# A new order for the steps behind the first 300, and a new deal of the PSUM banks, in linear attention with an MLP behind it

## Chip, cores, metric

The kernel runs on one core of one Trainium2 chip. The metric is the device time of one execution in microseconds, as a median of runs.

## What is computed

Softmax attention in its linear form, `q` over its feature axis and `k` over the sequence, for 8 batches of 8 heads, 576 positions of 64 features. Its output, as 4608 tokens of 512 features, goes through an MLP of width 2048 whose activation is `h * tanh(softplus(h))` (Mish). All in fp32.

```python
q_s = exp(q - max(q, -1)); q_s = q_s / (sum(q_s, -1) + 1e-09)
k_s = exp(k - max(k, 2));  k_s = k_s / (sum(k_s, 2) + 1e-09)
kv = einsum('bhsd,bhse->bhde', k_s, v)
attn = einsum('bhsd,bhde->bhse', q_s, kv)
x = attn.transpose(0, 2, 1, 3).reshape(4608, 512)
h = x @ w_in                                    # 512 x 2048
g = h * tanh(log1p(exp(minimum(h, 20.0))))
out = g @ w_out                                 # 2048 x 512
```

## The kernel before

Two heads make one item of 128 partitions, so there are 32 items, four to a batch. Every operand of the large matmuls is split into a high and a low part of a shorter fp32 form, and a product is three matmuls (high x high, high x low, low x high). All large matmuls have 128 rows, 128 columns of weights and 512 columns of data.

What is run, and when, stands in one string, `ORDER` (line 23): 2522 steps, each a name with numbers. Line 991 walks over it and calls the function that the table `stages` gives for the name. Scheduling is by hand, so each engine runs its instructions in the order of the steps, and waits by semaphores for what its next instruction reads, or for a buffer's last reader. `BANKS` (line 156) holds one letter for each PSUM tile in the order in which the steps allocate them; the letter names one of eight banks.

The steps that matter here, by engine:

- TensorE. `H n` (`h_part`, line 623): three matmuls of the first MLP product for one batch; `HM n`: four of these. `O`, `OP n.t` (`out_part`, line 667): three matmuls of the second MLP product into `po`. `A k.n.p` (`first_product`, line 815) and `BB k.f.p` (`second_product`, line 827): six matmuls each of the first and second MLP product for pairs of batches, in a form with seven products in place of eight (p = 1 to 7), into tiles `px`, `py`, `pz` and `qx`, `qy`, `qz`. `PX`, `PK`, `KP`, `XP`, `XT`, `T0` to `T7`: the small matmuls of the attention.
- VectorE. `RB`, `RC`: bit operations that decode the weights. `RD j`: the low part of a weight (`wi`, `wo`), a 128x512 subtract with both inputs in SBUF; `GL`: the same for `g`, with an input in PSUM. `WW`, `WL` (`w_whole`, line 720, `w_mix_lo`, line 745): adds and subtracts in SBUF that make mixed weights. `MK`, `MQ`, `Q`: maxima and sums of k and q; `KS`: the subtract of k's maximum; `U`, `T8` and up: transposes; `MT`, `KM`, `QV`: short steps in SBUF between them, `S`: the scaled `kv`. `GX`, `GK` (lines 872, 891), `XA`, `XL` (line 793): 128x1024 subtracts in SBUF that mix the data of the second form and make its low parts; a `BB` needs its `GK`, an `A` its `XL`. `J`, `DJ`: 128x512 adds out of PSUM.
- ScalarE. Exponentials, Mish, copies out of PSUM and all high parts (`RH`, `WH`, `GH`, `XH`, `C`, `N`, `Y`, `GM`, `EQ` and others).
- GpSimd. `SQ i`, `QM i` (lines 395, 494): q less its maximum, q times the inverse of its sum. `RO j`: low parts of weights, the rest that `RD` leaves. `RL`: a scaling; `WM` (line 728): mixed weights. `F e` (`w_fetch`, line 801): the DMA that fetches one tile of mixed weights for two products `A` or `BB`, 200 in all.
- SyncE issues all other DMAs: loads (`L`, `LK`, `LQ`, `V`, `R`), mixed weights to DRAM (`WK`, `WP`), and stores (`ST`, `ES`, `DS`, `DT`).

A fetch goes into one of six buffers in turn:

```python
RING = ["w0", "w1", "xa0", "xa1", "xa2", "xa3"]
tag = {2: "w14", 3: "w15"}.get(e, RING[(e - LEAD) % 6])
```

so `F e` waits, on GpSimd's queue, until the products of fetch e - 6 have been done, and all that stands behind it on that queue waits with it.

Of the kernel before, what the change touches and what calls it, by code (L numbers as in the profile page):

```python
# [47 lines left out]
GM20 WH13.1 MS10 T9 WL13.0 WL13.1 WW14v MT10 LK12 WP13.0 WP13.1 SQ10 WM14.0p WM14.1p PX8 PK8 Z9 Z8 EQ10 EV0.1s ZL9 S10
EV0.2v ZL8 Q10 MK12 QW10 WH14.0 ZT9 EV0.3s WH14.1 KB12 WK4 LQ11 QV10 WL14.0 WL14.1 KM12 MQ11 V12 WK12 WP14.1 WP14.0
WK13 WK14 HM30 HM26 HM31 HM16 HM18 HM17 HM22 MS11 UE12.0 QM10 T10 MT11 U12.0 WW15v SQ11 WM15.0p WM15.1p UE12.1 EQ11  # L50
Q11 QW11 GM30 GM26 WH15.0 WH15.1 ZT8 GM18 GM22 QV11 U12.1 WL15.0 WL15.1 LQ12 LK14 WP15.0 WP15.1 QM11 T11 WW0v WM0.0p
PX10 PK10 HM19 Z10 Z11 GM31 WM0.1p ZL11 ZL10 S12 MQ12 GM16 GM17 WH0.1 MS12 WH0.0 WL0.1 WL0.0 MK14 WW1v MT12 V14 ES0.2
# [1007 lines left out]
```

## Time and profile before

| | us |
|---|---|
| median of 3 runs (lowest, highest) | 795.55 (794.21, 798.1) |
| profiled execution | 794.31 |
| its span, first to last instruction | 792.5 |
| TensorE busy in it | 775.1 |
| VectorE, ScalarE, GpSimd busy | 565.6, 511.0, 295.1 |

TensorE ran at its full granted clock throughout. The profile is read from the waits of TensorE back: which wait ended last, which engine or DMA released it, and what stood in that engine's queue before. Busy shares are averages over stages with different limits. A large matmul is listed with some 0.39 us, but one follows the other every 0.23.

### The profile page before, as it was taken

What the parts mean: (1) busy time and instruction counts of PE and PEld (TensorE: products, weight loads), DVE (VectorE), ACT (ScalarE), POOL (GpSimd) and SP (SyncE); (2) the same over time, 40 slices, a digit from 0 to 9 for tenths busy, and PEclk for the clock granted to TensorE, in tenths of its full rate; (3) what the DMA queues carried; (4) which work ended last, traced back from release to release, by engine and by line L of the source; (5) the groups of instructions that cost most, each with busy time, mean ns of one, the idle gap of its engine ahead of it and who ended that gap; (6) DMA issues with size and microseconds to landing.
All of it is one profiled execution on the core that took longest, in us unless ns stands there. A gap on an engine that the chain in (4) does not pass through costs nothing.

```text
span 792.5 us, 12626 instructions
## 1 busy us (share of the span) xinstructions
PE 775.1 (98%) x4592; PEld 624.0 (79%) x4592; DVE 565.6 (71%) x877; ACT 511.0 (64%) x952; POOL 295.1 (37%) x378
## 2 busy tenths in 40 slices
...
GB/s 342 396 350 224 192 244 205 325 341 247 204 165 233 300 371 229 334 246 258 187 265 230 241 279 196 273 167 225 166 251 212 207 244 159 213 176 199 236 190 208
DMA packets 80717, 192.75 MB, mean 243 GB/s; under 512 B 16016, under 2 KB 28560, under 8 KB 80656
## 3 DMA queue, kind: packets, MB, share of 16 engines
...
q10 hardware_dynamic: 144, 0.13, 0.0%
...
## 4 chain that ended last, share of the span: by engine, by line
PE 68%; DVE 7%; DMA 7%; issue 2%; ACT 2%; POOL 1%; SPq 0%; POOLq 0%; ACTq 0%; DVEq 0%
PE px L823 14%; PE qx L839 13%; PE ph L629 11%; PE qz L839 9%; PE qy L839 8%; PE py L823 7%; PE pz L823 3%; DMA ws<-ws 3%; DVE gs L224 2%; DMA q<-in_qs_dram 2%; PE pt L573 1%; DVE g L224 1%; PE px L538 1%; PE po L670 1%; DMA xt_dram<-xt 1%
## 5 line engine op out<-in xcount | busy, mean ns | idle before, releaser
L807 POOL DMA_DIRECT2D ws<-ws x200 | 108.0, 542 | 350.1 <-PE qx L839 92.4
L224 DVE TENSOR_TENSOR gs<-g,gs 128x1024 fp32r<-128x1024 f32 x112 | 137.7, 1243 | 37.6 <-ACT gs L889 33.7
L889 ACT CAST gs<-g 128x1024 fp32r<-128x1024 f32 x112 | 116.7, 1051 | 62.8 <-PE qx L839 24.4
L839 PE MATMUL qx<-gs,ws 128*128 128x512 f32 x576 | 135.6, 391 | 0.4 <-DMA ws<-ws 0.4
L823 PE MATMUL px<-xh,ws 128*128 128x512 f32 x384 | 128.9, 393 | 2.6 <-DMA ws<-ws 2.4
L839 PEld LDWEIGHTS qx<-gs,ws 128*128 128x128 f32 x576 | 107.7, 188 | 24.8 <-DMA ws<-ws 0.8
L839 PE MATMUL qz<-gs,ws 128*128 128x512 f32 x384 | 92.0, 391 | 1.8 <-DVE gs L224 1.8
L629 PE MATMUL ph<-xs,wi 128*128 128x512 f32 x384 | 91.0, 393 | 1.3 <-DVE gl L224 1.0
L839 PE MATMUL qy<-gs,ws 128*128 128x512 f32 x384 | 90.8, 390 | 0.0
L859 ACT COPY g<-px 128x512 f32<-128x512 f32 x72 | 41.3, 586 | 76.0 <-PE px L823 68.2
L823 PEld LDWEIGHTS px<-xh,ws 128*128 128x128 f32 x384 | 72.1, 188 | 22.0 <-ACT g L859 2.3
L839 PEld LDWEIGHTS qz<-gs,ws 128*128 128x128 f32 x384 | 71.7, 188 | 18.8 <-DVE gs L224 2.2
L629 PEld LDWEIGHTS ph<-xs,wi 128*128 128x128 f32 x384 | 71.3, 188 | 19.0 <-DVE gl L224 1.4
L224 DVE TENSOR_TENSOR g<-g,g 128x1024 f32<-128x1024 f32 x64 | 78.6, 1241 | 9.1 <-ACT g L867 4.9
L839 PEld LDWEIGHTS qy<-gs,ws 128*128 128x128 f32 x384 | 72.0, 188 | 15.0
L823 PE MATMUL px<-xl,ws 128*128 128x512 f32 x192 | 74.9, 390 | 0.7 <-DVE xl L224 0.7
L863 DVE TENSOR_TENSOR g<-py,g 128x512 f32<-128x512 f32 x48 | 32.0, 681 | 56.3 <-ACT g L859 35.0
L823 PE MATMUL py<-xh,ws 128*128 128x512 f32 x192 | 65.9, 391 | 0.0
L224 POOL TENSOR_TENSOR q<-q,qm 128x576 f32<-128x576 f32 (+1 forms) x31 | 40.5, 1305 | 42.6 <-issue 18.4
L867 ACT ACTIVATE g<-g 128x512 f32<-128x512 f32 x72 | 43.1, 630 | 14.8 <-DVE g L863 14.6
L496 POOL TENSOR_TENSOR qe<-qe,qs 128x576 f32<-128x576 f32 x24 | 30.7, 1281 | 38.6 <-DVE qs L492 32.0
L629 PE MATMUL ph<-xs_odd,wi 128*128 128x512 f32 x192 | 44.9, 391 | 0.0
...
## 6 DMA issues: line engine op xcount, KB each, us to landing
ws<-ws POOLq DMA_DIRECT2D x197, 512.0 KB, 4.7
...
raw_out<-in_w_dram SPq DMA_DIRECT2D x14, 512.0 KB, 7.3
...
```

The costliest lines, as they stand in the source:

```text
L224: eng.tensor_tensor(out, a, b, ALU.subtract)
L496: eng.tensor_tensor(q2, q2, z.unsqueeze(2).to_broadcast(list(q2.shape)), ALU.mult)
L538: nc.tensor.matmul((px, pt)[x][h][o], kvt[a, j], at[e + j]["qT"][x][a], start=True, stop=True)
L573: nc.tensor.matmul(pkv[i][j * D:(j + 1) * D], k, v_two[a, j, c], start=c == 0, stop=c == NR - 1)
L629: nc.tensor.matmul(gs[n], wi[f][:, a, t], x[:, z], start=t == 0 and i == 0, stop=t == HP - 1 and i == 2)
L807: nc.gpsimd.dma_start(dst, src)
L823: nc.tensor.matmul(dst, w[:, a, j], xc[k, p][z][:, j].rearrange("p b s -> p (b s)"), start=p in (1, 2, 7) and j == 0 and i == 0, stop=j == ...
L839: nc.tensor.matmul(psb[key, k][m], w[:, a, m], g[z][:, f % 2], start=first and i == 0, stop=f == NH - 1 and i == 2, skip_group_check=p in ...
L859: nc.scalar.copy(g_quad(k, n)[q], psb[1, k, n])
L863: nc.vector.tensor_tensor(g, psb[2 if q == 0 else 7, k, n], g, ALU.add)
L867: nc.scalar.activation(g, psb[1, k, n] if q == 1 else g, AF.Mish)
L889: nc.scalar.copy(t[0], gq[k, h][G_PART[p]])
```

## The change

The first 300 steps of `ORDER` stay. The 2222 steps behind them, which begin at 57 us of the profiled execution, are the same steps in a new order, on every engine. The letters of `BANKS` are dealt anew from the 75th on, to go with that order. Nothing else differs: no step is added, removed or put on another engine. The order comes from a planner outside the kernel; here it was made anew with other assumptions: when VectorE and GpSimd want the port that they share, it goes to who asks first, and fetches are taken to land later.

The lines of the diff that hold the steps spoken of below:

```diff
--- before.py
+++ after.py
@@ -31,132 +31,132 @@
...
 RO13 RA17 RA14 RS17 RO12 QZ4 O3 RB14 RB17 Y5 RL23 GA5 RC17 Y6 RC14 RL19 GA6 H28 GL5 R25 O4 RS18 RA16 GL6 RA15 RH14
-RB16 RA18 RO14 R31 H29 H30 H31 RM21 QZ5 RC16 RB15 RC15 RH16 RA19 RA21 RH15 RH17 R26 RB19 RB21 RC19 QM4 RO16 RO17 QM5
...
-ZT5 RA27 RM27 Y9 GA9 RO25 WM8.0p RL28 WM8.1p GL10 RB27 GL9 RC27 MQ6 MK7 MK6 H44 H45 H46 H48 H47 H49 O7 B6 H50 H51 O8
-WH8.0 RH22 RH27 RA28 WH8.1 Y11 GA11 WL8.0 WL8.1 RD22 RB28 RC28 GL11 KS6 MQ7 WW9v WK6 WP8.0 LK8 WP8.1 RO26 RO27 SQ6 SQ7
...
-WK11 WP9.0 WP9.1 WK10 RO28 QM6 QM7 WM10.0p WM10.1p H52 H53 O9 H54 H55 H56 H57 H58 H59 O10 RW30 RH29 Y14 Y13 GA13 KB8
...
-WH11.1 Z6 Z7 U8.1 MT8 WL11.0 ZL7 WL11.1 ZL6 SQ8 RH30 EQ8 ST6 LK10 WP11.0 LQ9 WP11.1 ST5 ST7 RD30 Q8 WW12v MQ9 MK10
...
-KM10 MT9 WL12.0 QM8 SQ9 RO31 T8 UE10.1 UE10.0 EQ9 V10 WP12.0 WP12.1 LQ10 U10.0 Q9 WW13v QW9 OP14.0 HM28 HM20 HM23
...
-QV15 MT16 MK18 BB0.4.7 BB0.5.7 BB0.6.7 BB0.7.7 F14 F16 QM15 SQ16 F17 F15 T15 GK0.6.0 WL3.1 GX0.2.2v GX0.3.2v EQ16
-GH0.6.1 KB18 GH0.6.3 GH0.6.2 LQ17 WP3.0 V16 WP3.1 ST12 GK0.6.1 KM18 GX0.2.3v GK0.6.2 GK0.6.3 MQ17 Q16 DJ0.0.0 PX14
-BB0.0.6 BB0.1.6 BB0.2.6 BB0.3.6 BB0.4.6 GH0.3.0 XR14 GH0.5.0 XR15 UE18.1 QW16 MS17 UE18.0 BB0.5.6 BB0.6.6 PK14 BB0.7.6
-QV16 MT17 GK0.5.0 GK0.3.0 U18.0 F20 F19 F18 WM4.0p WM4.1p F22 F21 QM16 SQ17 GH0.5.1 DP0.2.0 DP0.2.1 ZT14 WH4.0 U18.1
...
-XL1.7 S20 XL1.2 XA1.3v XL1.6 A1.0.7 A1.1.7 A1.0.2 A1.0.6 F35 F37 F34 F36 DJ0.2.0 MQ20 WL5.1 XL1.5 WL5.0 DJ0.2.1 WP5.0
-WP5.1 DS0.2.1 DS0.1.0 DS0.3.1 DS0.0.1 DS0.2.0 PS C1.1.0 ZT19 XH1.4 MS20 C1.0.2 A1.1.2 A1.1.6 A1.2.1 A1.0.5 A1.2.2
-J1.1.0 MK22 J1.0.0 XL1.4 MT20 SQ20 F39 F38 C1.1.2 N1.1.0 KB22 C1.0.3 C1.2.0 EQ20 J1.2.0 J1.0.3 KM22 LQ21 A1.0.3 A1.1.5
...
-J2.0.0 QV28 XL2.6 MK30 XA2.3v XL2.5 BB1.5.4 A2.0.7 A2.1.1 BB1.6.4 BB1.7.4 A2.0.6 F90 QM28 F91 MS29 C2.1.0 XH2.4 KB30
-C2.0.2 A2.1.6 A2.1.2 A2.0.5 A2.1.7 DJ1.2.0 MT29 DJ1.2.1 T28 XL2.4 KM30 J2.1.0 SQ29 F92 F95 F94 F93 UE30.1 C2.1.2
...
-C3.0.2 F146 F144 F143 A3.1.2 BB2.6.4 A3.1.1 BB2.7.4 A3.0.5 F147 F145 F148 F150 F149 DJ2.2.1 DJ2.2.0 DJ2.1.1 DS2.2.0
-DS2.2.1 DS2.1.1 DS2.3.1 DS2.3.0 DS2.1.0 C3.1.0 C3.0.3 A3.2.1 A3.1.7 A3.1.6 A3.0.3 C3.2.0 C3.1.2 A3.1.5 A3.2.6 A3.2.2
...
-DS3.1.0 DS3.1.1 DS3.3.0 DS3.2.0 DT3.2.1.0
+RB16 RA18 RO14 RC16 RB15 RC15 H29 RH17 RA19 RM21 RH16 RH15 RA21 H30 H31 O5 RO17 RO16 RB19 RB18 RC19 RB21 RC18 RC21
...
+Y10 RM27 ZT5 ZT4 RA27 G10 GL10 RB27 MQ7 RC27 SQ6 WM8.0p WM8.1p SQ7 WH8.0 RH26 Y9 GA9 WH8.1 RH27 RH25 H44 H45 H46 B6
+H47 H48 WL8.1 WL8.0 KS6 GL9 RD22 WW9v R29 R28 LK8 ST5 WK1 WK10 WP8.0 WP8.1 WK3 WK9 RO25 RL28 RO26 WM9.0p WM9.1p RO27
+Y11 GA11 RA28 EQ6 EK6 EQ7 RA29 RM29 MK8 GL11 RB28 RC28 RB29 Q6 QZ6 Q7 O8 H49 O9 H50 H51 H52 H56 H57 H53 H54 H55 H58
+H59 O10 RH28 WH9.0 Y12 WH9.1 QZ7 WL9.0 RC29 WL9.1 WK11 WP9.0 WP9.1 RW30 KB8 RH29 GA12 Y13 GA13 Y14 GA14 KM8 WW10v GL12
+GL13 GL14 QM7 RO28 QM6 WM10.0p WM10.1p KP6 XP4 UE8.0 RW31 WH10.0 WH10.1 S6 U8.0 O11 T7 O12 WL10.0 WL10.1 RB30 RC30
+RB31 RC31 V8 WK4 WP10.0 WP10.1 LQ8 TC7 Z5 Z4 RH30 RD29 ZL5 ZL4 WW11v RD30 MQ8 T6 WM11.0p TC6 UE8.1 OP13.3 OP13.0 XP6
...
+Q8 WW12v OP14.3 OP13.2 OP13.1 H60 H61 OP14.2 PK6 OP14.1 HM23 H62 H63 QW8 Y15 GM23 QV8 S8 MK10 MQ9 WM12.0p WM12.1p QM8
...
+Q9 QW9 U10.0 QV9 U10.1 MQ10 WM13.0p QM9 WM13.1p HM19 HM24 OP14.0 HM28 HM20 OP15.2 OP15.3 OP15.0 OP15.1 PA WH13.0 GM28
...
+BB0.4.1 PK12 PX12 BB0.5.1 BB0.6.1 BB0.7.1 BB0.0.2 BB0.1.2 F7 SQ15 QM14 F8 F9 F10 GH0.2.1 GH0.2.2 XR13 XR12 S14 U16.0
...
+ES0.1 MK18 GX0.0.2v GK0.7.2 QV15 MQ16 KB18 ZT12 DP0.0.0 ZT13 WH3.1 DP0.0.1 GH0.7.3 MS16 F14 F13 WM4.0p QM15 DJ0.0.0
+GK0.7.3 GX0.3.2v MT16 WL3.1 T15 GX0.1.2v SQ16 F15 F16 EQ16 GH0.6.0 GH0.6.1 WH4.0 Q16 GK0.6.0 GX0.2.2v ST13 DS0.0.0
+WP3.1 ST12 LQ17 ES0.2 BB0.4.7 BB0.5.7 BB0.6.7 BB0.7.7 PX14 BB0.0.6 BB0.1.6 QW16 GH0.6.3 GH0.6.2 XR15 XR14 GH0.3.0 QV16
+GX0.3.3v GK0.6.1 GK0.6.3 DJ0.0.1 MQ17 GK0.6.2 KM18 PK14 BB0.2.6 BB0.3.6 BB0.4.6 BB0.5.6 UE18.0 UE18.1 GH0.5.0 ZT14
+MS17 GH0.5.1 F17 F19 F18 QM16 GX0.0.3v S16 GX0.2.3v GK0.3.0 MT17 GK0.5.0 T16 U18.0 U18.1 BB0.6.6 BB0.7.6 BB0.0.3 F20
+F21 F22 SQ17 WM4.1p F23 DP0.2.0 EQ17 DP0.2.1 ST14 LQ18 LK20 V18 BB0.1.3 BB0.0.5 BB0.1.5 Q17 GK0.5.1 WW5v BB0.2.5 WH4.1
...
+BB0.6.3 BB0.7.3 BB0.0.4 F26 F29 F28 F27 QM18 ZT17 MS19 XR16 XR17 ZT16 GH0.4.1 BB0.1.4 MT19 U20.0 U20.1 T18 GK0.4.1
+SQ19 BB0.2.4 GH0.4.2 EQ19 XH1.1 BB0.3.4 Q19 GK0.4.2 BB0.4.4 QW19 QV19 F31 QM19 F30 F33 F32 DJ0.1.0 S18 T19 PX18 XR19
...
+A1.0.1 BB0.5.4 BB0.6.4 BB0.7.4 A1.1.1 ZT19 XH1.7 XH1.2 C1.0.0 XH1.3 MK22 S20 XL1.7 XL1.3 XA1.2v XL1.2 KB22 ZT18 C1.1.0
+XH1.5 XH1.6 A1.0.7 A1.1.7 A1.1.2 A1.0.2 WM5.0p F35 F34 F37 WM5.1p XA1.3v XL1.6 KM22 DJ0.2.1 MQ20 XL1.5 A1.1.6 A1.0.6
...
+MS29 QW28 DJ1.2.0 KM30 XL2.4 MT29 DJ1.2.1 QV28 A2.1.6 A2.1.2 A2.1.7 A2.0.5 C2.1.2 UE30.0 C2.0.3 A2.1.5 A2.0.3 A2.2.1
+QM28 F93 SQ29 F94 F95 J2.0.3 T28 DJ1.1.1 J2.1.0 N2.0.1 C2.1.3 EQ29 C2.2.0 DS1.1.1 DS1.1.0 LQ30 ST26 A2.0.4 A2.2.2
...
+C3.0.2 C3.1.0 F144 F147 F145 F149 F146 F148 DJ2.2.1 DJ2.1.1 DJ2.2.0 XL3.5 DS2.1.1 DS2.3.0 DS2.2.0 DS2.1.0 DS2.2.1
...
 
 BANKS = """
-abcdefghadbcefga hebcfbagehdgabcg ehfdabchfbeahcfb hgdeaefcacaeaeae fcefecfaecaeface fefefaceefceafca eaefcaecfeaacefb
-aecbgfhedcbahdgb fcegbfadcfabhebc fegdhabcdfcbahah ahgehegfdaehgfcb fgbadghcafbdedef gcdabchfgaedfhga gaagbcagedbgfhbc
-fadaegacbadgfdcb bebfghcaedhcagfb echdbadeghdgbcfa cghghfdage
+abcdefghadbcefga hebcfbagehdgabcg ehfdabchfbeahcfb hgdeaefcacaeaeae fcefecfaecfcecea fecceacafeafceac fcfaecffcaeacefe
+cfbhgebfdcefbgdh caefdfcebgbhcedb ghfdeacgbhgceaae aedfdfbaehfdabcg aefhfgbcbehdbagh dfcabgecfdhdecaf faafbggbfahbecdh
+gfcagbegdfehcdge fabfgchaedahahbf gdcechfgabdecfhe fbgeadbfhg
```

## Rows read from the trace of the kernel before

**Rows 1.** The page: busy time of each engine, share of the span, instructions.
```profile
PE 775.1 (98%) x4592; PEld 624.0 (79%) x4592; DVE 565.6 (71%) x877; ACT 511.0 (64%) x952; POOL 295.1 (37%) x378
```

**Rows 2.** TensorE's waits: who waited for whom, total us, times, longest us.
```profile
PE px L823 <- DMA ws<-ws: 2.4, 2, 1.5
...
PE ph L629 <- DVE gl L224: 1.0, 1, 1.0
...
PE pq L515 <- DVE gl L224: 0.2, 1, 0.2
```

**Rows 3.** Windows: stretch, its length, busy us of each engine, clock, DMA.
```profile
57.40:121.30 63.90, 60.01 (x416) 45.25 (x415) 58.59 (x96) 49.42 (x95) 42.75 (x39) 1.00 0.67 229
234.70:318.70 84.00, 80.88 (x579) 63.35 (x578) 79.27 (x125) 56.90 (x114) 34.08 (x47) 1.00 0.84 280
```

**Rows 4.** VectorE's timeline, first stretch: start, us, line, operation, tiles, [idle before].
```profile
83.63 3.46 DVE L224 TENSOR_TENSOR m_out<-m_out 128x512 fp32r<-128x512 f32 x2 [0.37 <-POOL m_out L739]
87.01 1.75 DVE L224 TENSOR_TENSOR wo<-wc_out,wo 128x512 fp32r<-128x512 f32 x1
...
90.61 1.34 DVE L224 TENSOR_TENSOR k<-k,pb 128x1152 f32<-128x1152 f32 x1
91.87 0.81 DVE L392 TENSOR_REDUCE qm<-q 128x10 f32<-128x640 f32 x1
...
120.58 0.68 DVE L224 TENSOR_TENSOR wo<-wc_out,wo 128x512 fp32r<-128x512 f32 x1
```

**Rows 5.** GpSimd's timeline, first stretch.
```profile
84.80 1.74 POOL L224 TENSOR_TENSOR wi<-wc_in,wi 128x512 fp32r<-128x512 f32 x1
86.50 1.71 POOL L224 TENSOR_TENSOR q<-q,qm 128x640 f32<-128x640 f32 x1
```

**Rows 6.** VectorE's timeline, second stretch.
```profile
267.24 4.69 DVE L224 TENSOR_TENSOR gs<-g,gs 128x1024 fp32r<-128x1024 f32 x2
...
315.08 1.22 DVE L224 TENSOR_TENSOR xl<-raw,xh 128x1024 fp32r<-128x1024 f32 x1
```

**Rows 7.** GpSimd's timeline, second stretch.
```profile
268.54 1.18 POOL L496 TENSOR_TENSOR qe<-qe,qs 128x576 f32<-128x576 f32 x1
269.66 1.17 POOL L224 TENSOR_TENSOR q<-q,qm 128x576 f32<-128x576 f32 x1
```

**Rows 8.** TensorE's timeline where it had stood.
```profile
261.27 5.74 PE L839 MATMUL qx<-gs,ws 128*128 128x512 f32 x24 [0.40 <-DMA ws<-ws]
...
271.98 2.79 PE L839 MATMUL qz<-gs,ws 128*128 128x512 f32 x11 [1.83 <-DVE gs L224]
...
318.74 0.50 PE L823 MATMUL px<-xl,ws 128*128 128x512 f32 x1 [0.72 <-DVE xl L224]
...
497.56 0.47 PE L823 MATMUL px<-xh,ws 128*128 128x512 f32 x1 [0.92 <-DMA ws<-ws]
...
651.56 0.50 PE L823 MATMUL px<-xh,ws 128*128 128x512 f32 x1 [1.45 <-DMA ws<-ws]
```

**Rows 9.** TensorE's timeline, the first matmuls of `O9` and of `OP14.0`.
```profile
92.24 0.62 PE L670 MATMUL po<-wo,gh 128*128 128x512 f32 x2
...
124.46 0.62 PE L670 MATMUL po<-wo,gh 128*128 128x512 f32 x2
```

**Rows 10.** The chain that ended last: start, us, what; 36 matmuls without a break.
```profile
125.30 8.16 PE ph L629 x36
```

**Rows 11.** Groups by shape, 57 to 322 us: `MK`, xcount, busy us, mean ns, idle before.
```profile
L373 DVE TENSOR_REDUCE km<-kt_two 128x4 f32<-128x1152 f32 x7 | 9.3, 1329 | 0.0
```

**Rows 12.** GpSimd's timeline, the fetches F15, F93 and F149 (each last of its row).
```profile
254.04 1.12 POOL L807 DMA_DIRECT2D ws<-ws  x2
...
490.20 0.53 POOL L807 DMA_DIRECT2D ws<-ws  x1 [0.26 <-issue]
...
643.71 1.06 POOL L807 DMA_DIRECT2D ws<-ws  x2 [3.55 <-PE px L823]
```

**Rows 13.** The page's DMA issues: operation, count, KB each, median us to landing.
```profile
ws<-ws POOLq DMA_DIRECT2D x197, 512.0 KB, 4.7
```

More of the change, by code (lines that the diff above doesn't have):

```diff
@@ L48 @@
[L48 to L52, printed above, removed]
@@ L58 @@
-GM43 GM42 MQ14 GX0.0.0v GX0.0.1v QV13 GM47 MS14 F0 F1 F8 WM2.0p QM13 F3 WM2.1p T13 MT14 WW3v MK16 GX0.3.1v HM29 HM21
-HM25 BB0.0.1 BB0.1.1 BB0.2.1 HM27 BB0.3.1 SQ14 F6 F7 WH2.0 WH2.1 GM29 KB16 GM21 GH0.1.2 EQ14 GM27 GH0.2.1 GM25 GH0.2.0
-WL2.0 WL2.1 GX0.1.1v KM16 GK0.1.2 GX0.2.0v GX0.2.1v GK0.2.1 GK0.2.0 Q14 WP2.0 LQ15 ST11 WP2.1 UE16.1 QW14 UE16.0
-BB0.4.1 PX12 PK12 BB0.5.1 BB0.6.1 BB0.7.1 BB0.0.2 BB0.1.2 BB0.2.2 BB0.3.2 S14 QV14 MQ15 ZT13 ZT12 MS15 XR13 DP0.0.0
-GH0.2.2 XR12 GH0.7.0 GH0.2.3 GH0.7.1 WM3.0p WM3.1p QM14 F9 F11 F10 T14 WW4v MT15 GK0.2.2 U16.0 U16.1 GK0.2.3 GK0.7.0
@@ L73 @@
-BB0.6.3 PX16 BB0.7.3 BB0.0.4 BB0.1.4 UE20.0 QW18 UE20.1 GH0.4.1 MS19 GH0.4.2 QV18 GK0.4.1 MT19 F29 F27 WM5.0p QM18
-SQ19 F30 F28 F31 U20.0 T18 S18 GK0.4.2 WH5.0 EQ19 GH0.4.3 BB0.2.4 BB0.3.4 BB0.4.4 Q19 GK0.4.3 QW19 ZT17 XR17 XR16
-XH1.1 ZT16 QV19 F32 QM19 WM5.1p F33 DJ0.1.1 DJ0.1.0 T19 U20.1 XL1.1 XA1.0v ST17 DS0.3.0 LQ20 DS0.1.1 LK22 ST16 BB0.5.4
-PX18 PK18 BB0.6.4 A1.1.1 BB0.7.4 A1.0.1 XR19 XR18 XH1.3 XH1.2 XA1.1v XL1.3 XA1.2v XH1.7 XH1.6 ZT18 WH5.1 XH1.5 C1.0.0
-XL1.7 S20 XL1.2 XA1.3v XL1.6 A1.0.7 A1.1.7 A1.0.2 A1.0.6 F35 F37 F34 F36 DJ0.2.0 MQ20 WL5.1 XL1.5 WL5.0 DJ0.2.1 WP5.0
```

185 lines of the change are left out of this document (97 added, 88 removed).

## The prediction

> **What bounds the kernel now.** I read four views, from the whole down to single instructions. The page's head comes first: TensorE is busy for 775.1 us of a span of 792.5, on 4592 matmuls [rows 1]. Neither their number nor their shapes change, so the most that any order can win is what TensorE spends waiting. Next, TensorE's waits, summed by what ended them [rows 2]: leaving out the two groups that lie in the first 12 us, twelve groups sum to 9.5 us, from 2.4 down to 0.2. They fall into two kinds. Three waits for a fetched weight tile (`ws`, two in the group of 2.4 us and one of 0.4) make 2.8 us. Nearly all the rest, 6.4 us, are waits for VectorE, written as `gl`, `gs`, `xl` or `wc`.
>
> Why VectorE is late is seen in the windows: it is busy for 58.6 us of the 63.9 between 57.4 and 121.3, and for 79.3 of the 84.0 between 234.7 and 318.7 [rows 3]. In these two stretches VectorE sets the pace. Elsewhere it has air. Its timeline shows what it loses there beyond its own work. `WL8.0` and `WL8.1`, two 128x512 subtracts in SBUF that take 0.68 us each when undisturbed, as `RD30` does, took 3.46 together, and `RD22` of the same kind 1.75 [rows 4]; GpSimd was at `RO27` and `SQ6` meanwhile, and was stretched too, to 1.74 and 1.71 [rows 5]. Each blocked step cost VectorE some 1.07 us, and six of them make 6.2 us between 83 and 104. The worst is `GK0.3.0`, the second of two 128x1024 subtracts that took 4.69 us in place of 2.4 [rows 6]: GpSimd's `QM16` and `SQ17` ran back to back, 1.18 and 1.17 us, before VectorE came in [rows 7], and TensorE stood for 1.83 [rows 8].
>
> So the order is worth 9.5 us at most, and its worth is read at the points where VectorE or a fetch ends last, not from shares of busy time.
>
> **The change, part by part.** No step is added or removed: each engine runs the same instructions in another order, and banks are dealt anew. I therefore count, for each place that stalls now, which steps leave or join the queue ahead of it on TensorE and on the engine it waits for, at their durations here.
>
> *First stretch, at the output product `O9`.* `O9` needs `RD22`. Now `RD22` ends at 88.76 (87.01 + 1.75) and `O9` starts at 92.24, a margin of 3.5 us [rows 4, 9]. In the new order `H50` to `H53` no longer stand ahead of `O9`: four times three matmuls at 8.16/36 = 0.227 us, 2.7 us in all [rows 10]. On VectorE, `KS6` (1.34) and `MQ7` (0.81) now stand ahead of `RD22`, 2.15 us [rows 4]. The margin becomes 3.5 - 2.7 - 2.15 = -1.4 us. By then TensorE has now waited 2.1 us since the order departs (1.1 in short ones, and the 1.0 of `ph` for `gl`) [rows 2]; in the new order it would be 3.5 us. Now it goes on to 3.9 us by `OP13.2`, which is held by `RD29`. There, `WW11`, two adds, has moved from ahead of `RD29` to behind it and `U8.0`, one transpose, ahead of it, while TensorE's queue up to there holds the same steps; that is in VectorE's favour, so the place no longer adds. At the third place, product 14 behind `RD30`, 27 matmuls (6.1 us) and the short ones of `PK6`, which I put at 1.7, leave TensorE's queue; on VectorE seven steps leave, 4.4 us, most of them near the 0.68 of `RD30` itself. The margin now is 124.46 - 121.26 = 3.2 us [rows 4, 9], so it ends some 0.2 short. The stretch thus loses 3.5 to 4.2 us where it now loses 3.9: I take no change. This holds if the blocking by GpSimd costs VectorE as much as now. In the new order `SQ6` and `WM8` run before `WL8`, but `SQ7`, `RO25`, `RL28` and `RO26` stand beside `WL8`, `KS6` and `RD22`. The bounds are half of the present 6.2 us, which takes 3.1 from the stretch, and half as much again, which adds 3.1; as the number of GpSimd steps beside the blocked kind is about the same (three to four now, four then), I keep the present price.
>
> *Second stretch, at the mixes `XL1.2` and `XL1.6`.* TensorE now has waited 7.1 us when `XL1.6` has released it (the last 0.72 for `XL1.6`) [rows 8]. `MK22`, a maximum of 1.33 us [rows 11], moves ahead of `XL1.2` and `XL1.6`. `XL1.2` ended at 316.3 (315.08 + 1.22), just as its product began [rows 6], so 1.3 us more are waited there, on top of 6.3: 7.6. For `XL1.6` a product of 6 x 0.227 = 1.36 us has come ahead as well, so nothing is left of the shift. Against this, `QM16` and `SQ17` are parted: fetches and `QV16`'s followers now stand between them, so a subtract can be held by one of them, 1.18, and no longer by 2.35. VectorE has little idle time from there to `XL1.2`, so I let 1.2 us carry through (bounds 0 and 2.3). The stretch ends at 7.6 - 1.2 = 6.4 in place of 7.1: -0.7 us. It is a maximum and not a sum: VectorE's queue sets the time at its end, so what the fetch at 261 gives back, 0.40 us, is not added [rows 8].
>
> The Trainium skill, SBUF — State Buffer, section "SBUF: two separate sides", says that an operation that has the shared port pair keeps it for one whole instruction, and the other engine blocks for that long. By that alone, `GK0.3.0` would have lost at most 1.2 us. The trace shows two GpSimd instructions inside its one [rows 6, 7]; at the other place it agrees, since there `WL8.0` got its turn ahead of `RO27`, which was stretched by it [rows 4, 5].
>
> *Fetches.* Three now come late. F93 is issued at 490.20 and its product waits until 497.56, 0.92 us; F149 is issued as the second of the pair at 643.71, and its product waits until 651.56, 1.45 us [rows 8, 12]; F15 goes out as the second of the pair at 254.04, behind `QM15`, `SQ16` and F17, for 0.40 us. The median fetch takes 4.7 us to land [rows 13], these took some 7. I counted the TensorE work between the moment at which a fetch and all those ahead of it on GpSimd's queue have their buffers and its first use, at 1.36 us a product. For F93 that grows from 8.3 to 15.1 us, since it no longer stands behind F95 and F94; for F149 from 7.0 to 16.5; for F15 from 9.6 to 16.3. Over all fetches, 17 now have less than 7 us by their own buffer alone, the shortest 5.4; in the new order 8 do, the shortest 6.8. So the 2.4 us of F93 and F149 should go. Shorter than now become F92 (8.2 to 6.8), F147 (8.2 to 6.8) and F34 (8.6 to 7.2). They are bounded by 0, if they land as the median does, and by 0.9 us each, which is what a landing of 7.3 us (490.20 to 497.5) and an issue of 0.4 leave short. I take 0.4 us for all together.
>
> *Banks and stores.* A matmul group that takes a bank must wait for its last reader. The tightest such pairs now leave 1 to 1.5 us of TensorE work in between, eight of them, and 1.4 us, four of them, in the new order; they cost tenths now [rows 2] and I leave them as they are. Stores, loads on SyncE's queue and the last products and stores of the program keep their places to within a few steps; nothing waits for them now except one VectorE maximum, and I cost them at nothing.
>
> *Sum.* 0 - 0.7 - 2.4 + 0.4 = -2.7 us. The profiled execution took 794.31 us with its span of 792.5; the median of the runs is 795.55, 1.2 us above. I take the difference from the median: 792.9 us, with 791 to 795 as this case's own range.
>
> **The rivals.**
>
> *Meetings at the port become rarer.* For it: the six blocked steps of the first stretch and the four us of the second hang on a few tenths of a microsecond in where GpSimd starts; an order in which `SQ6` and `WM8` are done before `WL8` may miss half of them. Against it: `RO25` to `RO28` stand at the same blocked steps. Half of 6.2 and half of about 4 us would let the stretch end at 6.4 - 2.2 = 4.2; the total is 2.2 lower, 790.7.
>
> *GpSimd's pairs hold VectorE twice.* This one ends slower. `QM15` and `SQ16`, `SQ15` and `QM14`, `QM18` and `SQ19` stand next to each other in the new order with no fetch between, and VectorE's next steps behind `QV15`, `MT15` and `QV18` hold subtracts or short SBUF operations. The price of a held pair is 2.35 us [rows 7]; the place is the second stretch, where it goes to the end of `XL1.2` undiminished. One pair held is as now (6.4 becomes 7.6), and from two (9.9, with 2.4 of fetches won) the kernel is no longer faster. With three held and one meeting more at `RD22` it is 6.4 + 3 x 2.35 + 1.1 = 14.6 against 7.1, less 2.0 from fetches: +5.5, 801.0. Of the two prices, the second stretch speaks for the dearer and the first for the cheaper [rows 5, 7]. By the rule of the Trainium skill named above (SBUF — State Buffer) a pair could hold only for one of its instructions, 1.2 us each, and the end would be 6.4 + 3.6 = 10.0, 796.5 us.
>
> *Fetches land late all the same.* The change doesn't do what it says: F92, F147 or those behind `QM19` wait as F93 and F149 did. Then the 2.4 us stay, 795.3.
>
> **How the numbers follow.** Forecast 0.48, rarer meetings 0.28, late fetches 0.10, held pairs 0.14. The range reaches 1.7 us below the case of rarer meetings, 789.0, and at the upper end to two pairs held with one meeting more (9.9 + 1.1 for 7.1, the fetches' 2.0 off, +1.9) and some two us of fetches that land late on top, 798.8; it leaves out about a tenth on either side. What this measurement can tell from no change is 0.5%, 4 us: faster means below 791.6, slower above 799.5. Rarer meetings are faster in 0.26, the forecast's lower edge in 0.08: 0.34. Held pairs are slower in 0.12. The rest, 0.54, lies within.
>
> **What would show it.** TensorE's waits of the new kernel should hold no `ws` of over 0.5 us; if they do, the fetch step is wrong. `O9` should be released by `RD22` (written `po <- wo`), with 3 to 4 us waited up to there; if far less, meetings became rarer. Between 235 and 320, VectorE should have no 128x1024 subtract above 2.5 us; one above 3 is a held pair. Busy time of TensorE should stay at 775 us, else the whole frame is wrong.

## The result: 788.1 us, faster than forecast

The new order took 788.13 us (median of five runs, 787.28 to 789.09) against 795.55 of the kernel before; ratio 0.990, 95% interval 0.986 to 0.993. The forecast was 792.9, its range began at 789.0. The profiled execution has a span of 785.5 us, against 792.5.

The page's busy line and TensorE's waits answer to [rows 1, 2]: TensorE's work is nearly the same (773.4 us against 775.1), and the waits for VectorE have shrunk. Without the two groups of the first 12 us, the waits sum to 5.8 us, against 9.5. The largest group is now the one I expected to vanish, fetched weights.

```profile
PE 773.4 (98%) x4592; PEld 623.5 (79%) x4592; DVE 560.6 (71%) x877; ACT 516.7 (66%) x958; POOL 298.3 (38%) x378
...
PE px L823 <- DMA ws<-ws: 2.0, 2, 1.3
...
PE pkv L573 <- DVE gl L224: 1.2, 1, 1.2
...
PE qy L839 <- DVE gs L224: 0.8, 1, 0.8
```

To see where the 7.0 us came from I measured TensorE's *lag* at the same steps in every trace: the start of a step, less the start that it would have if TensorE had run without a break since `H29` (at 58 us), each step at its duration in the kernel before. A stall adds to it, and so does a step that runs longer. Below zero means only that steps ran some tenths shorter than before, often those that had held a wait there. Two executions of the new kernel (the last but one row repeats it) agree within 0.35 us up to 320 us. The rows marked * are experiments told below.

| kernel | lag at `O9` | `O12` | `PX8` | `BB0.0.6` | `A1.0.5` | `A2.0.1` | last product | span | median, us | ratio to before, 95% |
|---|---|---|---|---|---|---|---|---|---|---|
| before | 2.1 | 3.8 | 3.9 | 3.9 | 7.05 | 7.3 | 9.7 | 792.5 | 795.55 | |
| new | -0.2 | 0.7 | 0.4 | 0.9 | -0.35 | 4.2 | 4.1 | 785.5 | 788.13 | 0.986 to 0.993 |
| first free * | 0.9 | 0.85 | 1.2 | 2.3 | 5.0 | 5.3 | 7.8 | 790.2 | 792.0 | 0.994 to 0.997 |
| price back * | -0.2 | 1.6 | 1.2 | 1.8 | 0.0 | 5.1 | 5.0 | 786.9 | 789.16 | 0.992 to 0.996 |
| first, then old * | -0.2 | 0.7 | 0.2 | 0.9 | 3.5 | 3.7 | 6.4 | 790.2 | 790.57 | 0.990 to 0.996 |
| second only * | 2.1 | 5.0 | 5.5 | 6.0 | 4.7 | 7.8 | 10.4 | 792.7 | 795.53 | 0.997 to 1.001 |
| pair narrow * | 2.1 | 3.9 | 4.0 | 4.9 | 6.4 | 6.6 | 9.4 | 791.8 | 793.72 | 0.996 to 0.999 |
| steps swapped * | 2.1 | 3.85 | 3.9 | 3.7 | 8.1 | 8.7 | 14.2 | 796.8 | 794.26 | 0.996 to 1.000 |
| tail only * | 2.1 | 3.9 | 3.8 | 3.7 | 6.3 | 12.3 | 12.8 | 794.1 | 796.92 | 0.999 to 1.004 |
| new, again * | -0.2 | 0.7 | 0.2 | 0.9 | -0.4 | 3.5 | 3.45 | 785.3 | 788.23 | 0.990 to 0.993 |
| new, mended * | -0.1 | 0.7 | 0.25 | 0.9 | 0.1 | 1.6 | 1.6 | 783.4 | 785.1 | 0.986 to 0.989 |

New against before, piece by piece: the first stretch (to `PX8`) -3.5; from there to `A1.0.5`, the second stretch, -3.9 (3.2 then, -0.8 now); from there to `A2.0.1` +4.2; from there to the end -2.4; the start, up to `H29`, -0.9, though its steps are the same (57.7 to 59.7 us over all runs: an accident); -0.5 is in none of these.

One part of the first stretch has nothing to do with the port. In the kernel before, TensorE waits 1.0 us for VectorE between 66 and 69 us, where no step of VectorE is held yet. In the new kernel 0.1 of this is left. TensorE's timeline of before:

```profile
67.84 0.30 PE L516 MATMUL pqt<-ident,q 128*128 128x128 f32 x1 [0.63 <-DVE wc_in L276]
68.35 3.04 PE L629 MATMUL ph<-xs,wi 128*128 128x512 f32 x12 [0.20 <-DVE wc_out L276]
```

I call a step *held* if it takes longer than the same step does when it is undisturbed. The first stretch, VectorE's timeline of the new kernel (start, us, line, operation, tiles, count, [idle before]); it answers to [rows 4]:

```profile
82.26 1.29 DVE L224 TENSOR_TENSOR m_out<-m_out 128x512 fp32r<-128x512 f32 x2 [1.23 <-ACT m_out L743]
83.47 1.35 DVE L224 TENSOR_TENSOR k<-k,pb 128x1152 f32<-128x1152 f32 x1
84.74 0.69 DVE L224 TENSOR_TENSOR gl<-ph,gh 128x512 fp32r<-128x512 f32 x1
85.34 0.68 DVE L224 TENSOR_TENSOR wo<-wc_out,wo 128x512 fp32r<-128x512 f32 x1
85.94 2.38 DVE L726 TENSOR_TENSOR w_out<-wo 128x512 f32<-128x512 f32 x2
```

And GpSimd's beside it, for [rows 5]:

```profile
80.80 1.26 POOL L224 TENSOR_TENSOR q<-q,qm 128x640 f32<-128x640 f32 x1
83.35 1.36 POOL L224 TENSOR_TENSOR wi<-wc_in,wi 128x512 fp32r<-128x512 f32 x1 [1.29 <-ACT wi L289]
84.80 1.57 POOL L261 TENSOR_SCALAR raw_out<-raw_out 128x512 uint32<-128x512 uint32 x1
86.45 1.32 POOL L224 TENSOR_TENSOR wo<-wc_out,wo 128x512 fp32r<-128x512 f32 x1
```

The two `WL8` take 1.29 us together (3.46 before) and `RD22` 0.68 (1.75): none is held. The first held step is the second `WW9`, behind `RD22`. In the second stretch `GK0.3.0` and `GK0.5.0` of VectorE stand singly, at 1.22, and it is GpSimd's `SQ17` that is stretched, to 1.64; before, both lay in one row of 4.69 [rows 6, 7]:

```profile
263.15 1.22 DVE L224 TENSOR_TENSOR gs<-g,gs 128x1024 fp32r<-128x1024 f32 x1
...
264.37 1.22 DVE L224 TENSOR_TENSOR gs<-g,gs 128x1024 fp32r<-128x1024 f32 x1
...
264.97 1.64 POOL L224 TENSOR_TENSOR q<-q,qm 128x576 f32<-128x576 f32 x1
```

What was given back: TensorE's timeline at two new waits for fetches, F36 and F39, then GpSimd's queue that issued them, and then a place at 411 to 417 where VectorE is late for TensorE, which stood in no row of before:

```profile
322.22 0.47 PE L823 MATMUL px<-xh,ws 128*128 128x512 f32 x1 [0.66 <-DMA ws<-ws]
...
327.92 0.47 PE L823 MATMUL px<-xh,ws 128*128 128x512 f32 x1 [1.33 <-DMA ws<-ws]
...
314.59 0.57 POOL L807 DMA_DIRECT2D ws<-ws  x1
315.18 1.18 POOL L224 TENSOR_TENSOR q<-q,qm 128x576 f32<-128x576 f32 x1
317.87 1.10 POOL L807 DMA_DIRECT2D ws<-ws  x2 [1.51 <-PE px L823]
...
411.65 3.41 DVE L224 TENSOR_TENSOR g<-g,g 128x1024 f32<-128x1024 f32 x2
414.99 0.74 DVE L392 TENSOR_REDUCE qm<-q 128x18 f32<-128x576 f32 x1
...
416.92 5.53 PE L839 MATMUL qy<-gs,ws 128*128 128x512 f32 x23 [0.76 <-DVE gs L224]
```

### The profile page after: what moved, and what is told of

Same layout as the page of the kernel before. It is cut to its first block, busy times and chain, and to the rows that moved or that the text cites. A ratio compares the mean times of both kernels' runs of the same rounds, so it can differ in the third digit from the quotient of the medians.

```text
span 785.5 us, 12653 instructions
## 1 busy us (share of the span) xinstructions
PE 773.4 (98%) x4592; PEld 623.5 (79%) x4592; DVE 560.6 (71%) x877; ACT 516.7 (66%) x958; POOL 298.3 (38%) x378
## 4 chain that ended last, share of the span: by engine, by line
PE 75%; DVE 9%; ACT 8%; DMA 3%; issue 3%; POOL 1%; SPq 0%; DVEq 0%; ACTq 0%; POOLq 0%
PE qx L839 15%; PE px L823 14%; PE ph L629 10%; PE qz L839 10%; PE qy L839 9%; PE py L823 7%; PE pz L823 3%; PE px L538 2%; PE po L670 1%; PE pt L573 1%; DMA ws<-ws 1%; DVE gs L224 1%; DVE g L224 1%; DVE wa L269 1%; DVE w_out L726 1%
## 5 line engine op out<-in xcount | busy, mean ns | idle before, releaser
L863 DVE TENSOR_TENSOR g<-py,g 128x512 f32<-128x512 f32 x48 | 32.4, 683 | 57.7 <-PE py L823 29.6
```

Of the source, the lines that this page charges most:

```text
L863: nc.vector.tensor_tensor(g, psb[2 if q == 0 else 7, k, n], g, ALU.add)
```

## The experiments

Three theories to begin with. (A) The meetings of VectorE and GpSimd at the port became fewer where TensorE waits, and what is won in one stretch is kept in the next. (B) The order of VectorE's queue won the time, or the second stretch is a bound of its own, as I had reckoned. (C) The fetches did it. The edits are shown shortened. In them, `old` and `new` are the two orders; a *seam* is a place where a run changes from one order to the other, and the PSUM banks behind it were dealt anew.

**The price of the first stretch, taken away.** The price is the time that VectorE loses in held steps. `RO26` and `RO27` become plain copies on ScalarE, and `SQ6` leaves out most of its tile.

```diff
- sub(eng, d[1], a, d[0].bitcast(F32))           # RO
+ nc.scalar.copy(d[1], a) if j in (26, 27) else sub(eng, d[1], a, d[0].bitcast(F32))
+ if i == 6: qt, qm = qt[:, 0:1], qm[:, 0:1]     # SQ6
```

> The old kernel, but in the first stretch the three GpSimd steps that held VectorE don't: SQ6 works on the first row of its tile only, and RO26 and RO27 are plain copies on ScalarE (so what is computed is wrong in both), all at their places in the order. No step of VectorE moves and none waits for a GpSimd step that comes later. (A) If the meetings cost TensorE time: WL8.0, WL8.1 and RD22 take 0.68 us each, RD22 ends at about 85.6, the wait of ph for gl at 89.4 goes (lag at O9 1.1 instead of 2.1), and of the 1.7 us waited for gl at 102 to 105 at least half goes: lag at O12 1.1 to 2.0 instead of 3.8, span 1.8 to 2.7 us under before. (B) If the order of VectorE's queue decides, lag at O12 stays over 3.3. (D) If VectorE has air between 89 and 102, lag at O9 1.1 and at O12 about 2.8.

VectorE's timeline, and TensorE's one short wait that was left in the place of three:

```profile
83.30 1.37 DVE L224 TENSOR_TENSOR m_out<-m_out 128x512 fp32r<-128x512 f32 x2 [0.38 <-POOL m_out L744]
84.59 0.68 DVE L224 TENSOR_TENSOR wo<-wc_out,wo 128x512 fp32r<-128x512 f32 x1
...
101.81 1.97 PE L543 MATMUL px<-qT,kvt 64*64 64x512 f32 x8 [0.23 <-DVE gl L224]
```

Lag at `O12` 0.85 instead of 3.8: of the 3.2 us that GpSimd took from VectorE in `WL8.0`, `WL8.1` and `RD22`, TensorE gets 3.0 back, without one step of VectorE moved. (A) holds here. Lag at `O9` is 0.9, as the short waits at 66 to 69 are still there. 1.5 us were lost again by `BB0.0.6`, 0.9 of this around a wait for VectorE's transposes at 158 us, which some executions of the old order show and some don't.

**The price put back into the new order.**

```diff
- RO25 RL28 RO26 WM9.0p WM9.1p .. RO27
+ RO26 RO27 RO25 RL28 WM9.0p WM9.1p ..
```

> The new kernel with one change, on GpSimd alone: RO26 and RO27, whose inputs are ready at 80.6 and 82.8 us, stand ahead of RO25 and RL28. GpSimd so works on two-input steps from about 82 to 86 us, while VectorE does WL8.1, WL8.0, KS6, GL9 and RD22. In the new kernel none of these was held, and RD22 ended 0.09 us before O9 began. (A) The order of VectorE's steps leaves O9 no margin and the gain there is the price of the meetings: two or three steps are held again for 1.07 us each, RD22 ends at 87 to 89 instead of 86.0, TensorE's lag at O9 is 1 to 3 us instead of -0.2, at O12 1.5 to 3.5 instead of 0.7, and the median is 1 to 3 us above that of the new kernel. (B) VectorE's new order has won the time: lag at O9 below 0.5, median as the new kernel. (E) VectorE asks first all the same and GpSimd is the one that waits: no held step before RD22, nothing changes.

VectorE's timeline, then TensorE inside `O9`:

```profile
82.65 3.30 DVE L224 TENSOR_TENSOR m_out<-m_out 128x512 fp32r<-128x512 f32 x2 [1.22 <-ACT m_out L743]
...
87.73 0.67 DVE L224 TENSOR_TENSOR wo<-wc_out,wo 128x512 fp32r<-128x512 f32 x1
88.33 1.28 DVE L726 TENSOR_TENSOR w_out<-wo 128x512 f32<-128x512 f32 x2
...
88.46 0.50 PE L670 MATMUL po<-wo,gh 128*128 128x512 f32 x1 [1.57 <-DVE wo L224]
```

Two steps are held again for 2.0 us, and TensorE stands for `RD22` within `O9`. But `WW9`, which the new kernel had held for 1.1, is free, so VectorE is 0.9 later on balance. The lag at `O12` is 0.9 higher, and so is the median (789.16 against 788.23 in the runs beside it; lowest and highest 788.61 and 790.91 against 787.15 and 788.91, so they overlap).

This is not (A) alone. By what I had written down, the lag at `O9` should have been 1 to 3 us, and it stayed at -0.2, as (B) wanted; the time rose, as (A) wanted, but by less than 1 us. The whole stretch shows both. Its held steps cost VectorE 5.9 us before, 4.6 here and 3.7 in the new kernel; the lag at `O12` is 3.8, 1.6 and 0.7. With 1.3 us of price less than before the lag is 2.2 lower. The other 0.9 is not the port's: it is about what the short waits at 66 to 69 made (lag at `O9` 0.9 with the price taken from the old order, -0.2 in the new order with the price and without). So of the 3.1 us won up to `O12`, some 2 are (A) and some 1 is the new order itself, or its banks; no run parts these two.

**The meetings avoided by moving steps.** Two versions of the old order.

```diff
- RO26 RO27 SQ6 SQ7        # old
+ SQ7 RO26 RO27 SQ6        # all three later
+ SQ6 SQ7 RO26 RO27        # two later
```

> The old kernel with one change: on GpSimd RO26, RO27 and SQ6 stand behind SQ7, which waits for MQ7. GpSimd so stands still while VectorE does WL8.0, WL8.1 and RD22, which it held for 3.2 us between 83.6 and 88.8. VectorE's own order is untouched. (A) If it is the meetings: WL8.0, WL8.1 and RD22 take 0.68 us each, RD22 ends at about 85.5 instead of 88.8, the wait of ph for gl at 89.4 (0.97 us) goes, and TensorE's lag at O12 (3.8) is 1 to 3 us less; the span is 1 to 3 us under before unless the moved steps meet VectorE later. (B) If it is the order of VectorE's queue (GL9 and GL11 against RD22, KS6, MQ7): lag at O9 and O12 as before, within 0.3 us. A price that only moves shows as meetings of 1.07 us between 89 and 121, and a lag at O12 as before in spite of an early RD22.

> The old kernel with RO26 and RO27 moved behind SQ7 on GpSimd; SQ6, which Q6 needs through ScalarE, now comes first and keeps its place in time. (A) Meetings at the port decide: SQ6 meets WL8.0 (1.76 us), WL8.1 and RD22 take 0.68 us each, RD22 ends at about 86.6 instead of 88.8, the wait of ph for gl at 89.4 (0.97 us) goes and TensorE's lag at O9 is about 1.1 instead of 2.1; at O12 it is 1.7 to 2.8 instead of 3.8, more if RO26 and RO27 meet VectorE between 92 and 96. Span 1 to 2 us under before. (B) The order of VectorE's own steps decides: lag at O9 2.1, as before.

Lag at `O9` was 0.9 and 0.8, near what (A) had, and 6.8 and 5.8 at `O12`: 798.5 us (ratio 1.001 to 1.006) and 796.6 (0.999 to 1.003). In the first, VectorE's `Q6` waits for the `SQ6` that I had moved back; in the second, `RO26` and `RO27` delay `WM9`, and VectorE stands with `WL9` at the head of its queue, then TensorE:

```profile
97.75 2.36 DVE L224 TENSOR_TENSOR m_out<-m_out 128x512 fp32r<-128x512 f32 x2 [2.56 <-POOL m_out L739]
...
102.58 1.89 PE L573 MATMUL pkv<-v,k 64*64 64x66 f32 x70 [2.02 <-DVE gl L224]
```

A meeting avoided by making the GpSimd step late is paid for at the step that needs its result: TensorE's wait at 103 was 2.27 and 2.02 us instead of 0.74. More was lost behind it. TensorE's waits up to `O12` sum to 4.5 and 3.5 us, against 3.8 before; the other 2.3 and 2.2 us of lag are steps that ran longer at a lower clock (last section).

**New first stretch, old second.**

```diff
- ORDER = old
+ ORDER = new[0:960] + [s for s in old if s not in new[0:960]]
```

> The first 960 steps new (up to about 237 us, the first stretch and the long middle), then the old order, so that the second stretch of the old kernel is met some 3 us earlier by TensorE than before. (A) VectorE's work there follows TensorE, so the stretch costs what it cost before: lag 0.9 us at BB0.0.6 and about 4.1 at A1.0.5 (0.9 + 3.2), span 789 to 790. (B) The stretch is a bound of its own, as my prediction reckoned: what was won is waited back, lag at A1.0.5 about 6 to 7 us, span 792 to 793.

TensorE's timeline at the wait for `GK0.3.0`, [rows 8] of before:

```profile
269.18 3.11 PE L838 MATMUL qz<-gs,ws 128*128 128x512 f32 x9 [1.83 <-DVE gs L223]
```

The lag rises by 2.6 us in the old stretch, met 3 us earlier, where it rose by 3.2, with the same 1.83 in it. That the two are so near is chance. TensorE's waits here are 1.9 us instead of 3.2: those for the fetch at 261 and for `xl` are gone. But right behind the wait the granted clock fell, and 1.6 us of the lag are two products that ran longer. The window shows it (columns as in [rows 3]; before, it stood at 1.00 here):

```profile
270.00:274.00 4.00, 4.00 (x12) 3.17 (x11) 4.00 (x6) 1.46 (x2) 0.00 (x0) 0.57 0.58 164
```

Nothing that was won is waited back: (B), a bound of its own, is out. (A)'s size, "what it cost before", was met by luck. The same with the seam at step 680 doesn't bear on this: I had dealt `HM30` a bank that VectorE's `ZL9` reads late, TensorE stood for 9.4 us and the kernel took 804.9.

> The first 680 steps of the new order (up to the product of head pair 8 at about 141 us), then the rest in the old order. Three theories. (A) The meetings at the port became fewer in the first stretch, and what VectorE is late there is carried into the second stretch: TensorE's lag at PX8 falls from 3.9 us to about 0.4, the wait at BB0.0.5 for gs (1.8 us at 272 before) shrinks too, and the span is 3.5 to 5.5 us under that of before (787 to 789 against 792.5). (B) The second stretch is a bound of its own, as my prediction reckoned: what the first stretch wins, TensorE waits back at 272 and 319, and the span is within 0.7 us of before. (C) The fetches did it: the lag at PX8 is unchanged, 3.9 us.

**Old first stretch, new second.** `old[0:680]`, `new` up to 1270, the rest old.

> The first 680 steps old, the steps from 680 to 1270 (some 141 to 325 us, the second stretch with its fetches) new, the rest old. (A) The stretch's own meetings, above all the pair at GK0.3.0, cost TensorE about 1.8 to 3 us, and these go: TensorE's lag rises from 3.9 us at PX8 to no more than 5 at A1.0.5 (7.05 before); behind that the late fetches of the new order cost up to 2 us. Span 1 to 3 us under before. (B) VectorE's lateness alone decides and the new order of the stretch is worth 0.7 us: lag at A1.0.5 about 6.3, span 0 to 1 us under before. (C) By the fetches alone: the waits on ws at 322 and 328 us appear (2.0 us), the span is 0 to 2 us longer than before.

The lag falls by 1.3 between `BB0.0.6` and `A1.0.5`, as in the new kernel, though TensorE is 5 us later; before, it rose by 3.2. The stretch's own worth is thus 4.4 us. In the new kernel 2.8 of the 4.4 are waits that went (3.2 before, 0.4 now), and 1.6 are steps that ran shorter, 1.0 of it in the four products that had held these waits. But 2.8 are lost behind the stretch, at my seam at step 1270, 2.0 of it in one wait for VectorE and only 0.4 in one for a fetch, and 1.2 had been lost at 105 in a spell of lower clock (last section), so the time is that of before. TensorE's timeline at the seam:

```profile
335.04 0.50 PE L822 MATMUL pz<-xh,ws 128*128 128x512 f32 x1 [1.96 <-DVE g L862]
```

Of (C) nothing is left here but 0.4.

**The pair alone, made short.** `QM16` and `SQ17` leave out most of their tiles.

```diff
+ if i == 16: q2, z = q2[:, 0:1], z[:, 0:1]        # QM16
+ if i == 17: qt, qm = qt[:, 0:1], qm[:, 0:1]      # SQ17
```

> The old kernel, but GpSimd's QM16 and SQ17 work on the first row of their tile only (the rest is left out, so head 16's and 17's results are not those wanted): the pair stays in its place in every queue, and only its time at the port goes. GK0.3.0 should take 1.2 instead of 3.55 us. (A) The price of the pair goes through to TensorE: the wait at 272 us (1.83) goes, lag at A1.0.5 4.7 to 5.3 instead of 7.05, span 1.8 to 2.3 us under before. (B) The price is swallowed behind it, by VectorE's idle time before XL1.2 and XL1.6 or by waits there: lag at A1.0.5 over 6.3.

`GK0.5.0` and `GK0.3.0` in one row of VectorE's timeline:

```profile
267.59 2.39 DVE L224 TENSOR_TENSOR gs<-g,gs 128x1024 fp32r<-128x1024 f32 x2
```

The wait at 272 is gone: between `BB0.0.3` and `BB0.4.3` the lag falls by 0.3 where it rose by 1.8. From `BB0.0.6` to `A1.0.5` it rises by 1.5 instead of 3.2, so 1.7 of the pair's 2.3 us arrive. By the bounds that I had written down this is (B): lag at `A1.0.5` 6.4, and a span only 0.7 us under before. But 1.0 us of that lag had come in ahead of the pair, by `BB0.0.6`. Counted from there, 2.1 us arrive up to `BB0.4.3`, nearer (A); part of it is lost again behind it, where the small matmuls `PX18` and `PK18` at 303 to 306 ran 0.8 us longer.

**The pair given to another step.**

```diff
- GK0.5.0 GK0.3.0
+ GK0.3.0 GK0.5.0
```

> The old kernel with two steps of VectorE exchanged: GK0.3.0 ahead of GK0.5.0. GpSimd's pair QM16 and SQ17 then should hold GK0.5.0 (3.5 us) and leave GK0.3.0 at 1.2 us; VectorE's work and the price at the port are the same, but TensorE needs GK0.3.0 first (BB0.0.3, BB0.1.3) and GK0.5.0 2.7 us later. (A) The wait of 1.8 us at 272 goes and doesn't come back: lag at A1.0.5 about 5.2 instead of 7.05, span 1.5 to 2 us under before. (B) VectorE is no earlier at XL1.2 and XL1.6, and TensorE waits there for xl what it won: lag at A1.0.5 7.0, span as before within 0.4 us.

VectorE, then TensorE:

```profile
267.77 4.70 DVE L224 TENSOR_TENSOR gs<-g,gs 128x1024 fp32r<-128x1024 f32 x2
...
276.84 8.51 PE L839 MATMUL qx<-gs,ws 128*128 128x512 f32 x35 [0.71 <-DVE gs L224]
...
286.91 0.43 PE L538 MATMUL pt<-qTt,kvt 64*64 64x64 f32 x4 [0.20 <-DVE kvt L589]
287.69 0.27 PE L538 MATMUL pt<-odd,kvt 64*64 64x64 f32 x2 [0.36 <-DVE odd L510]
```

Both theories missed. The wait at 272 went, but the price stayed with VectorE and TensorE met it at the next three steps: 1.8 us between `BB0.0.3` and `BB0.4.3`, as before. So inside the stretch VectorE's sum of work seems to decide, and not which step is held. (This profiled execution was its kernel's slowest; the interval says no change.)

**The tail alone.** `old[0:1270]`, the rest new.

> The first 1270 steps old, the rest new: the fetches F93 and F149, for which TensorE waits 0.92 and 1.45 us, come earlier, and nothing of the two bound stretches is touched. (A) The two waits go (2.4 us), and the new waits on VectorE at 407 to 425 us, seen in the new kernel (2.2 us), come in their place: span within 1 us of before. (C) If the fetches are what made the kernel faster, the span is 2.4 to 5 us under before. TensorE's lag up to A1.0.5 is as before in both, 7.0 us.

With F93 and F149 earlier, the lag rises 0.5 from `A2.0.1` to the last product instead of 2.4. The waits at 407 to 425 cost 2.2, as in the new kernel; a wait of 1.9 for ScalarE at my seam, a spell of lower clock behind it and what else lies between `A1.0.5` and `A1.2.4` cost 3.9. TensorE's timeline at the seam:

```profile
335.52 0.55 PE L823 MATMUL px<-xh,ws 128*128 128x512 f32 x1 [1.90 <-ACT g L859]
```

The fetches are thus worth about 2 us, and by themselves they don't make the kernel faster: (C) is out at 796.9 us.

**The new kernel, mended.** One version moves F36 and F39 forward and takes the steps from 1436 to 1700 out of the old order.

> The new kernel up to step 1436 and from step 1700 on, and the old order from 1436 to 1700 (some 381 to 461 us), so that the three waits on VectorE at 407 to 425 us, which only the new kernel has (2.2 us), go; besides F36 and F39 are issued right behind A1.0.6 and A1.1.6, ahead of SQ20 and F38, and A1.0.6 and A1.0.4 one step earlier on TensorE, so that the waits for ws at 322 and 328 (2.0 us) go. If stretches and fetches each cost what their own order makes them cost, the lag at the end is about 0 instead of 4.1 us, the span about 781 us and the median about 783.5 (0.985 of before). If F36 and F39 land later because of the stores and loads that run then, not because of their place in the queue, 1 to 2 us of this stay: 783 and 785.5.

The two waits for `ws` went, but at the seams TensorE stood 3.0 and 2.0 us for ScalarE, for a bank and for `xh`, and the time was 795.2:

```profile
390.24 0.50 PE L823 MATMUL px<-xh,ws 128*128 128x512 f32 x1 [3.01 <-ACT g L859]
```

The other only moves single steps within the new order:

```diff
- F35 F34 F37 WM5.1p .. A1.1.6 A1.0.6 .. F36 SQ20 F38 F39
+ F35 F34 F37 .. A1.0.6 F36 WM5.1p A1.1.6 F39 .. SQ20 F38
- GX1.3.1v MQ26 .. XR22 GH1.7.2 .. GK1.7.2
+ GX1.3.1v XR22 GH1.7.2 GK1.7.2 MQ26
- GX1.2.2v GX1.3.2v T25
+ T25 GX1.2.2v GX1.3.2v
```

> The new kernel with its own new waits mended by moves of a few places: A1.0.6 ahead of A1.1.6 on TensorE, so that F36's buffer is free 1.4 us sooner; F36 issued ahead of WM5.1p, F39 ahead of SQ20 and F38; GK1.7.2 ahead of MQ26, and T25 ahead of GX1.2.2v and GX1.3.2v. No steps of the old order are taken back and no PSUM bank changes. If the new waits are matters of place in a queue: the waits for ws at 322 and 328 us (2.0 us) go, the waits at 416 (0.76, gs) and 425 (0.53, qT) fall below 0.3, the lag at the end falls from 4.1 to about 1 us, the span to about 782.5 and the median to about 785. If F36 and F39 are late because of the stores and loads of that time, 1 us or more of the waits for ws stays: 784 and 786.5. If the waits on VectorE only move to the next step, the lag between BB1.0.7 and BB1.0.4 still rises by 2 us.

GpSimd's queue with F36 and F39, and TensorE's waits for fetches in the whole kernel:

```profile
313.50 0.53 POOL L807 DMA_DIRECT2D ws<-ws  x1 [0.29 <-issue]
...
315.42 0.57 POOL L807 DMA_DIRECT2D ws<-ws  x1
...
PE px L823 <- DMA ws<-ws: 0.4, 1, 0.4
```

785.1 us (784.88 to 785.55), the fastest of all. Both waits for `ws` at 322 and 328 are gone; the 0.4 that is left stands at 642. So F36 and F39 were late by their places on GpSimd's and TensorE's queues, not by the stores and loads of that time, which are the same. A wait for ScalarE at 316, 0.3 us in the new kernel, grew to 0.85. Between `BB1.0.7` and `BB1.0.4` 1.7 of 2.2 us stay: the waits at 416 and 425 went, and smaller ones came behind them. The new kernel in the same form as given, beside the price put back:

> The new kernel as it is, beside the kernel before on the same chip and in the same call as the run with the price put back. Its median is 788.1 us from five runs, with a range of 1.8 us, against 795.8 with a range of 9 for the kernel before. If the gain is that of the profiled executions (785.5 against 792.5 us of span), the ratio is about 0.991; if the executions of before that are slower than the profiled one add to it, as spells of a lower clock at 100 to 110 us would, it is about 0.990 and the range of the new kernel stays under 3 us.

It ran at 788.23 (787.15 to 788.91), ratio 0.992, as its profiled span has it.

## Why the prediction was wrong, step by step

*What bounds it.* TensorE's work stayed near 775 us and most was won and lost in its waits: right in the main. The waits fell by 3.7 us (9.5 to 5.8) and the lag by 5.6; the other 1.9 are steps that ran shorter, which no term held.

*`O9` and the first stretch: no change.* Measured -3.5. Two steps failed: I kept the price at the port, and I carried over the 1.1 us of short waits ahead of `O9`, which the new kernel doesn't have. The margin at `O9` was right but for these: short by 1.4 with the price in `RD22`, it has 1.8 to spare without these 3.2 us, and TensorE, 2.3 earlier, uses about that up: `RD22` ended 0.09 us before `O9` began. I kept the price of 6.2 (its six steps sum to 5.9) because as many GpSimd steps stood beside the blocked kind. What counts is which of them run at the time: `SQ6` had run by 77 us, `SQ7` by 82, `RO25` waited for ScalarE until 83.35, and the step beside `RD22` was `RL28`, which doesn't hold it. In the whole stretch 3.7 us were lost by four steps instead of 5.9 by six, none of the four ahead of `RD22`, and the lag rose by only 0.9 from `O9` to `O12`. My rival of rarer meetings was this, and it had a chance of 0.28. Its half of the price (3.1 us) was even somewhat more than went (2.2); its time of 790.7 was too long all the same, since it let only 2.2 us of its two halves (3.1 and 2) come through, by the maximum below.

*The second stretch: -0.7.* Measured -3.9. The terms were mis-sized: the parted pair, 1.2, gave 1.7 by itself, and 2.1 up to `BB0.4.3`; the 1.3 us that I charged for `MK22` do not show, as no wait for `xl` of 0.2 us or more is left; 0.4 us came back from the fetch at 261, which I did not add; and 1.6 us are steps that ran shorter. Behind the terms stands a step that failed too, "a maximum and not a sum": I took VectorE's times at the end of the stretch as fixed, so that nothing won ahead of it could arrive. The old stretch behind the new first one shows the contrary: it began 3 us earlier, and TensorE waited less in it than before, 1.9 us, not more. VectorE's work in it starts when TensorE's products feed it.

*Fetches: -2.4 + 0.4.* F93 and F149 came as forecast (2.4). The other side was 2.0 instead of 0.4, and in fetches that I had not named. I counted from the moment at which the buffers of a fetch and of all fetches ahead of it are free. F39's was free at 312.8, but ahead of it on its queue stood also `SQ20`, and F38, which waited for TensorE until 317.87. The median landing of 4.7 us [rows 13] was no help either: F36 went out at 314.59 and its product began at 322.22.

*What no term held.* At 407 to 425 us VectorE "has air", I wrote, and took the places outside the two stretches as free. Measured: 2.2 us, with two 128x1024 subtracts held (`GX1.3.1`, `GX1.2.2`) and a maximum, `MQ26`, ahead of the `GK1.7.2` that TensorE needed.

*Held pairs.* No VectorE subtract between 235 and 320 took over 1.8 us: that rival is out. "Late fetches" was true in kind and too small to decide.

*The sum.* What fell short behind 320 us, some 1.6 in fetches and 2.2 at 407 to 425, hid part of what the two stretches had won beyond the forecast, 3.5 and 3.2. With the -2.7 of the forecast, -3.5 - 3.2 + 1.6 + 2.2 makes the -5.6 by which the lag fell; the rest of the 7.4 between the medians is the start (0.9 in the profiled executions) and what differs between executions. The mended kernel, with much of this put right, ran at 785.1. The upper end of my range doesn't add up either: 1.9 and 2 us above 795.55 are 799.4 and not 798.8, but nothing came near it.
